# A decode kernel's last weights: w_down cut into sixteen blocks, the second half of wo into six pieces

## The chip, the core and the metric

The kernel runs on one core of one Trainium2 chip. The metric is device time in microseconds of one execution. Three unprofiled runs of the kernel before took 1313.51, 1313.98 and 1314.48 us; their median, 1313.98 us, is the time before.

## What is computed

One token of each of four sequences goes through an attention block with a cached history and, beside it, through a gated feed-forward block; a learned gate mixes the two. All data are 32-bit floats. Cut to what matters:

```python
# x [4, 1, 512]; k_cache, v_cache [4, 32, 4096, 128]; wq [512, 4096]; wo [4096, 512]
# w_gate, w_up [512, 1792]; w_down [1792, 512]; gate_w [512]
g = sigmoid((x * gate_w).sum(-1, keepdims=True))
q = (x @ wq) split into 32 heads of 128
p = softmax(q @ k_cache^T / sqrt(128))
a = (p @ v_cache, heads joined) @ wo
b = (gelu_tanh(x @ w_gate) * (x @ w_up)) @ w_down
out = g * a + (1 - g) * b
```

The two caches are 268 MB each, so nearly all of the 565 MB that the kernel reads is cache.

## The kernel before

**Tiles.** A tile is four heads of one sequence: 4096 positions of four heads lie as 128 partitions by 128 positions by 128 numbers, 64 KB in each partition, 8 MB in all. There are NT = 32 such tiles of K and 32 of V. Everything that comes from memory lands in one large array, `big`, whose stretches are reused: `K(i)` and `V(i)` give the stretch for tile i, and neighbouring K tiles overlap in a quarter, which is why each K tile is worked through in a `shared` quarter and a remaining three quarters. VectorE multiplies K by the query (`products`, L213) and sums (`sums`, L219), ScalarE makes the exponentials (`soft_max`, L237 and L240), TensorE multiplies by V (`pv`, L272).

**Order.** The order of the instructions is written out by hand (`tc.manual_schedule()`), engine by engine in program order. Every load is issued by SyncE's queue (SP), in program order: an issue that must wait for a stretch of `big` to become free holds back all issues behind it. The loop issues K(i+1) after the first quarter of tile i has been summed, and V(i) after `pv(i-1)`.

**The feed-forward block.** Up and gate projections run in the first tile of the loop (`ffn_up`, `ffn_gelu`). The result lies as 128 partitions by 448 columns: partition group j of 32 holds the rows of x for the features j·448 to j·448+447. VectorE transposes it in 14 strided selections of 32 columns (L349), so that `hT[:, i, :]` holds feature 14p+i in partition p. That fits `load_d` (L88), which puts rows 14p to 14p+13 of w_down into partition p as one run of 28 KB.

**The end.** After the loop SP issues `load_d`, then `load_w(0)` (L95, heads 0 to 15 of wo, 16 rows of 2 KB in each partition, in two pieces) and `load_w(1)` (heads 16 to 31, in four pieces of 9, 4, 2 and 1 rows, as `WO_END` says). w_down and the first half of wo go into the stretch of V(30), which `pv(30)` frees; the second half of wo goes into the stretch of K(31), which the last `sums` frees. TensorE then does, in this order: `pv(31)`, the gathering of the last heads, `ffn_down` (into `wide`, L254), the transposes of `turn(1)` (L307), the sixteen products of wo's first half (also into `wide`), `fold` (ScalarE copies `wide`, L264, and TensorE adds its four groups into `acc`), and the sixteen products of wo's second half (into `acc`, L259, four each). VectorE copies `acc` out (L413) and SP stores it (L414).

Of the kernel before, what the change touches and what calls it, by code (L numbers as in the profile page):

```python
# [9 lines left out]
F32 = mybir.dt.float32  # L10
# [7 lines left out]
def tile_gated_mix(ctx: ExitStack, tc: tile.TileContext, x, kc, vc, wq, wo, w_gate, w_up, w_down, gate_w, out):  # L18
    nc = tc.nc
    P = 128  # L20
    B, H, S, D = kc.shape
    DM = x.shape[2]
    F = w_gate.shape[1]
# [9 lines left out]
    RJ = 4  # L33
    BP = 2
    FG = F // 4
    FC = F // P
    HW = 16
    E = HW * D // P
    GW = HW // HT
    WO_END = ((0, E // 2, E), (0, 9, 13, 15, E))  # L40
    scale = 1.0 / math.sqrt(D)
    c_gelu = math.sqrt(2.0 / math.pi)

# [8 lines left out]
    consts = ctx.enter_context(tc.tile_pool(name="consts", bufs=1))  # L52
# [9 lines left out]
    big = kv.tile([P, VA + TW], F32)  # L62
    Q0, F0, F1, W0, D0 = VA, VA, VA + KC * F, VA, VA + TW // 2
    W1, ES = TW, TW + TW // 2

    def place(a, n):
        return big[:, a:a + n]
# [17 lines left out]
        nc.sync.dma_start(place((F0, F1)[s], KC * F), (w_gate, w_up)[s].rearrange("(p c) n -> p (c n)", c=KC))  # L85

    def load_d():
        nc.sync.dma_start(place(D0, FC * DM), w_down.rearrange("(p i) n -> p (i n)", i=FC))  # L88

    def load_w(w):  # L90
        t = place((W0, W1)[w], E * DM)
        src = wo[w * HW * D:(w + 1) * HW * D].rearrange("(p e) n -> p (e n)", e=E)
        ends = WO_END[w]
        for e0, e1 in zip(ends, ends[1:]):
# [149 lines left out]

    acc = ps1.tile([P, C4], F32, name="acc")
    wide = ps1.tile([P, DM], F32, name="wide")
    NW = FC + E
    nw = iter(range(NW))


    def project_wide(t, w):
        n = next(nw)
        c = n % 4
        nc.tensor.matmul(wide[32 * c:32 * c + 32, :], t, w, start=n < 4, stop=n >= NW - 4)  # L254

# [69 lines left out]


    hT = consts.tile([P, FC, 32], F32)
    fu = place(VA + 2 * KC * F, 2 * DM).rearrange("p (s n) -> p s n", s=2)

    def ffn_up(s):  # L330
# [7 lines left out]
    def ffn_gelu():  # L338
        x1 = fu[:, 0, :FG]
        t1, t2, t3, th, y, v = (place(F1 + a * DM, FG) for a in range(6))  # L340
        nc.vector.tensor_tensor(t1, x1, x1, op=OP.mult)  # L341
        nc.vector.tensor_scalar(t2, t1, 0.044715, 1.0, op0=OP.mult, op1=OP.add)  # L342
        nc.vector.tensor_tensor(t3, t2, x1, op=OP.mult)  # L343
        nc.scalar.activation(th, t3, AF.Tanh, scale=c_gelu)  # L344
        nc.vector.scalar_tensor_tensor(y, th, 1.0, x1, op0=OP.add, op1=OP.mult)  # L345
        nc.vector.scalar_tensor_tensor(v, y, half, fu[:, 1, :FG], op0=OP.mult, op1=OP.mult)  # L346

        for i in range(FC):
            nc.vector.transpose(hT[:, i, :], v[:, i::FC])  # L349

    def ffn_down():
        for f in range(FC):
            project_wide(hT[:, f, :], place(D0 + f * DM, DM))


    load_f(0)
# [2 lines left out]
    for i in range(NT):  # L359
# [12 lines left out]
        if i == 0:  # L372
            half, gmask = gates()
            ffn_up(0)
            ffn_up(1)
            ffn_gelu()
            load_v(0)
# [14 lines left out]
        if b == 1 and g + 1 < NG:  # L392
            q_spread(g + 1)
    load_d()
    load_w(0)
    load_w(1)
# [4 lines left out]
    gather(NG - 1)  # L401
    weigh(NG - 1)
    ffn_down()
    turn(1)
    turned(1)
# [31 lines left out]
```

## Time and profile before

| what | us |
|---|---|
| median of three runs (lowest, highest) | 1313.98 (1313.51, 1314.48) |
| the profiled execution, its own time | 1314.19 |
| its span, from the first instruction to the last | 1312.4 |
| DMA in the span: 565.07 MB, mean rate | 431 GB/s |
| VectorE busy, share of the span | 1143.1, 87% |
| TensorE busy, share of the span | 394.1, 30% |
| w_down, from issue to landing | 18.1 |
| the four pieces of wo's second half, from issue to landing | 27.8 (first), 30.6 and 30.7 (last two) |

The profile's page and the answers of the trace give times from the start of the span; the profiled execution lasted 1.8 us longer than its span. A window's row gives, in this order: the stretch, its length, the busy time and number of instructions of PE (TensorE matmul), PEld (weight load), DVE (VectorE), ACT (ScalarE) and POOL, the granted TensorE clock, the busy share of the 16 DMA engines and what they moved. A row of the timeline has start, duration, engine, line, operation, output and inputs with shapes, and in brackets how long the engine had been idle and what ended that.

### The profile page before, as it was taken

The numbers are of one execution on the slowest core, as the hardware profiler recorded it, in microseconds if no ns is written. First come the engines' busy times: TensorE is split into PE (matmuls) and PEld (weight loads), VectorE is DVE, ScalarE is ACT, GpSimd is POOL, SyncE is SP. The second block draws the span as 40 slices with busy tenths as digits, with TensorE's granted clock in tenths as the row PEclk, the third lists the DMA queues.
The fourth block names the chain that finished last, engine by engine and source line by source line (L and its number), as shares of the span: only waits on it lengthen the run. The fifth ranks groups of instructions, "written<-read, shape, count | busy, mean of one in ns | idle before, by whom it ended". The sixth has DMA issues, their size and how long they took to land.

```text
span 1312.4 us, 6364 instructions
## 1 busy us (share of the span) xinstructions
PE 394.1 (30%) x2728; PEld 132.3 (10%) x2728; DVE 1143.1 (87%) x261; ACT 92.7 (7%) x321; POOL 0.7 (0%) x6
## 2 busy tenths in 40 slices
PE   2403323322233221333232233322123332123237
PEld 0100001000011000100011000100001000010003
DVE  1799989988899988988989988998889899898890
ACT  0010000000000100000000000000000000000010
POOL 0000000000000000000000000000000000000000
PEclk9656666556666655666655666665566665566668
DMA  9999999999999999999999999999999999999997
GB/s 416 432 432 440 423 440 423 442 433 435 436 428 435 434 433 435 436 431 430 434 442 430 436 428 437 432 433 438 429 439 424 442 431 434 441 422 440 431 426 335
DMA packets 10855, 565.07 MB, mean 431 GB/s; under 512 B 1336, under 2 KB 1352, under 8 KB 1612
## 3 DMA queue, kind: packets, MB, share of 16 engines
q1 hardware_dynamic: 10828, 564.68, 99.4%
q8 instruction: 21, 0.34, 0.1%
q14 instruction: 6, 0.05, 0.0%
HBM read 564.67 MB, written 0.01 MB: 430 GB/s over the span
## 4 chain that ended last, share of the span: by engine, by line
DMA 71%; DVE 28%; PE 0%; issue 0%; SPq 0%; ACT 0%; DVEq 0%
DMA big<-in_A_k_cache 69%; DVE big L213 14%; DVE sc L219 14%; DMA big<-in_A_wo 2%; PE acc L259 0%; DVE m L233 0%; DVE hT L349 0%; DVE big L346 0%; DVE big L341 0%; DVE big L343 0%; DVE big L345 0%; ACT big L344 0%; DVE m L226 0%; DVE t L313 0%; DVE big L342 0%
## 5 line engine op out<-in xcount | busy, mean ns | idle before, releaser
L213 DVE TENSOR_TENSOR big<-big,qb 128x4096 f32<-128x4096 f32 x64 | 555.8, 8684 | 104.2 <-DMA big<-in_A_k_cache 104.2
L219 DVE TENSOR_REDUCE sc<-big 128x32 f32<-128x4096 f32 x64 | 555.4, 8678 | 1.1
L272 PE MATMUL po<-big,PM 128*32 128x512 f32 x2048 | 296.0, 743 | 437.0 <-DMA big<-in_A_v_cache 434.6
L272 PEld LDWEIGHTS po<-big,PM 128*32 128x32 f32 x2048 | 80.7, 133 | 626.0 <-issue 623.5
L235 PE MATMUL sm<-m,ones 1*128 1x4 f32 x64 | 18.7, 360 | 217.9 <-DVE m L233 217.9
L228 PE MATMUL sm<-ident,m 128*1 128x128 f32 x32 | 11.9, 371 | 213.9 <-DVE m L226 180.2
L240 ACT ACTIVATE PM<-sc,nb 32x128 f32<-32x128 f32 x128 | 67.4, 526 | 2.5
L237 ACT ACTIVATE nb<-sm 128x4 f32<-128x4 f32 x32 | 5.6, 174 | 570.8 <-PE sm L235 570.8
L235 PEld LDWEIGHTS sm<-m,ones 1*128 1x128 f32 x64 | 15.9, 306 | 237.6 <-DVE m L233 237.6
L281 ACT ACTIVATE o<-po 128x512 f32<-128x512 f32 x16 | 9.6, 597 | 324.2 <-PE po L272 324.2
L228 PEld LDWEIGHTS sm<-ident,m 128*1 128x1 f32 x32 | 2.5, 79 | 236.4 <-issue 183.3
L240 ACT ACTIVATION_READ_ACCUMULATOR PM<-sc,nb 32x1 f32 x128 | 26.2, 205 | 0.0
L200 ACT ACTIVATE qb<-q 128x512 f32<-128x512 f32 x8 | 4.8, 597 | 245.3 <-PE q L196 245.3
L128 DVE COPY xT<-sm 128x128 f32<-128x128 f32 x4 | 0.9, 282 | 20.4 <-PE sm L125 20.4
L196 PE MATMUL q<-QM,hmask 128*32 128x512 f32 x64 | 14.6, 1004 | 3.5 <-DVE QM L186 3.5
L289 PE MATMUL sm<-o,sel 128*16 128x128 f32 x128 | 15.6, 273 | 0.0
L334 PE MATMUL q<-big,xT 128*32 128x448 f32 x64 | 10.4, 813 | 9.3 <-DMA big<-in_B_w_gate 4.9
L299 DVE RECIPROCAL ri<-sm 16x1 f32<-16x1 f32 x8 | 1.2, 147 | 13.4 <-PE sm L291 13.4
L289 PEld LDWEIGHTS sm<-o,sel 128*16 128x16 f32 x128 | 11.7, 97 | 7.4 <-issue 5.0
L413 DVE COPY res<-acc 128x128 f32<-128x128 f32 x1 | 0.3, 291 | 13.2 <-PE acc L259 13.2
L226 DVE TENSOR_REDUCE m<-sc 128x1 f32<-128x128 f32 x32 | 9.2, 286 | 1.1
L233 DVE TENSOR_REDUCE m<-sm 1x4 f32<-1x128 f32 x32 | 8.7, 272 | 0.6 <-PE sm L228 0.6
(61 smaller groups left out, 79.2 us busy)
## 6 DMA issues: line engine op xcount, KB each, us to landing
big<-in_A_wo SPq DMA_DIRECT2D x2, 2048.0 KB, 25.0
big<-in_B_w_gate SPq DMA_DIRECT2D x1, 3584.0 KB
big<-in_B_w_up SPq DMA_DIRECT2D x1, 3584.0 KB, 27.6
big<-in_B_w_down SPq DMA_DIRECT2D x1, 3584.0 KB, 18.1
big<-in_A_wo SPq DMA_DIRECT2D x1, 2304.0 KB, 27.8
big<-in_A_wo SPq DMA_DIRECT2D x1, 1024.0 KB
big<-in_A_k_cache SPq DMA_DIRECT2D x32, 29.6
big<-in_A_v_cache SPq DMA_DIRECT2D x32, 29.2
```

Of the source, the lines that this page charges most:

```text
L196: nc.tensor.matmul(ps[h * PH:(h + 1) * PH].rearrange("p b d -> p (b d)"), hmask[:, j, a:a + 1].to_broadcast([P, PH]), QM.rearrange("p b d ...
L213: nc.vector.tensor_tensor(t, t, QB[g][:, b:b + 1, :].to_broadcast([P, r1 - r0, D]), op=OP.mult)
L219: nc.vector.tensor_reduce(SC[i][:, r0:r1], K(i).rearrange("p (r d) -> p r d", d=D)[:, r0:r1], axis=AX.X, op=OP.add)
L226: nc.vector.tensor_reduce(m1, SC[i], axis=AX.X, op=OP.max)
L228: nc.tensor.transpose(MT[i], m1, ident)
L233: nc.vector.tensor_reduce(m2, MT[i].rearrange("o (h p) -> o h p", h=HT), axis=AX.X, op=OP.max)
L235: nc.tensor.matmul(nbp, ones[:1, :], m2, start=True, stop=True)
L240: nc.scalar.activation(PM[:, PZ:].rearrange("p (c m) -> p c m", m=32)[s, :, h:RJ * HT:HT], SC[i][s, :].rearrange("p (c j) -> p c j", j=RJ) ...
L272: nc.tensor.matmul(PO[i // BP % 2][32 * c:32 * c + 32].rearrange("p j d -> p (j d)"), PM[:, m0:m0 + 32], V(i)[:, j * N:(j + 1) * N], start ...
L281: nc.scalar.activation(O[i // BP], PO[i // BP % 2], AF.Copy)
L289: nc.tensor.matmul(OS[g][:, :D], sel[:, j, m0:m0 + B * HT], O[N * g + n][:, j, :], start=(n, j) == (0, 0), stop=(n, j) == (N - 1, RJ - 1))
L334: nc.tensor.matmul(ps[32 * j:32 * j + 32, :], xT[:, c, :32], place((F0, F1)[s] + c * F + j * FG, FG), start=c == 0, stop=c == KC - 1)
```

## The change

w_down's 1792 rows are seen as NE = 16 blocks of FB = 112 rows. Block e belongs to partitions 8e to 8e+7. Of each block the first 96 rows are loaded as before, as one load of all blocks, 12 consecutive rows in each of the 8 partitions (24 KB a partition). The last 16 rows of each block come by two more loads, one for blocks 0 to 7 and one for blocks 8 to 15, 2 rows in each of 8 partitions for each block. Both of these loads go to partitions 0 to 63, side by side in a free stretch at the end of K(31)'s place (`DX`). So partitions 0 to 63 receive 16 rows each, and partitions 64 to 127 receive 12, where all received 14.

The transposes and the products follow: 12 transposes and products over 128 partitions, and 4 over 64 (`hX`), in place of 14 over 128. The second half of wo comes in pieces of 4, 4, 3, 2, 2 and 1 rows in place of 9, 4, 2 and 1.

```diff
-    FC = F // P
+    NE, EP = 16, 8
+    FB = F // NE
+    XR = 2
+    FC = FB // EP - XR
+    XP, XC = P // 2, 2 * XR
...
-    WO_END = ((0, E // 2, E), (0, 9, 13, 15, E))
+    WO_END = ((0, E // 2, E), (0, 4, 8, 11, 13, 15, E))
...
+    DX = ES + 4 * DM
...
     def load_d():
-        nc.sync.dma_start(place(D0, FC * DM), w_down.rearrange("(p i) n -> p (i n)", i=FC))
+        blocks = w_down.rearrange("(e f) n -> e f n", f=FB)
+        nc.sync.dma_start(place(D0, FC * DM), blocks[:, :EP * FC].rearrange("e (p i) n -> e p (i n)", i=FC))
+        for k in range(2):
+            nc.sync.dma_start(place(DX + k * XR * DM, XR * DM)[:XP],
+                              blocks[k * EP:(k + 1) * EP, EP * FC:].rearrange("e (p i) n -> e p (i n)", i=XR))
...
-    NW = FC + E
+    NW = FC + XC + E
...
+    hX = consts.tile([XP, XC, 32], F32)
...
+        v = v.rearrange("r (e f) -> r e f", f=FB)
+        main = v[:, :, :EP * FC].rearrange("r e (p i) -> r e p i", i=FC)
+        rest = v[:, :, EP * FC:].rearrange("r e (p i) -> r e p i", i=XR)
         for i in range(FC):
-            nc.vector.transpose(hT[:, i, :], v[:, i::FC])
+            nc.vector.transpose(hT[:, i, :], main[:, :, :, i])
+        for k in range(2):
+            for i in range(XR):
+                nc.vector.transpose(hX[:, k * XR + i, :], rest[k * XP:(k + 1) * XP, :, :, i])
...
     def ffn_down():
         for f in range(FC):
             project_wide(hT[:, f, :], place(D0 + f * DM, DM))
+        for f in range(XC):
+            project_wide(hX[:, f, :], place(DX + f * DM, DM)[:XP])
```

## The prediction

> **What bounds the kernel now.** I read the page first: the span, the DMA row of the 40 slices and the queue table, then the chain of waits.
>
> ```profile
> span 1312.4 us, 6364 instructions
> DMA  9999999999999999999999999999999999999997
> q1 hardware_dynamic: 10828, 564.68, 99.4%
> q8 instruction: 21, 0.34, 0.1%
> DMA 71%; DVE 28%; PE 0%; issue 0%; SPq 0%; ACT 0%; DVEq 0%
> ```
>
> The DMA engines are full from the first slice to the last but one. VectorE's 28% of the chain is no second bound: it passes between the landing of one K tile and the issue of the next, while the engines still work off a V tile. The windows give the rate, in the bulk and while w_down arrives.
>
> ```profile
> 135.70:1256.50 1120.80, 322.36 (x2133) 104.81 (x2133) 1020.70 (x191) 78.86 (x282) 0.00 (x0) 0.62 1.00 434
> 1280.20:1288.60 8.40, 8.20 (x64) 2.21 (x65) 0.00 (x0) 0.15 (x2) 0.00 (x0) 0.82 0.98 421
> ```
>
> 434 GB/s over 16 engines is 27.1 GB/s for one. The change moves the same bytes, so only two things can alter the time: how evenly the engines finish, and whether the new loads keep that rate. The end, in windows of 1 us:
>
> ```profile
> 1302.00:1303.00 1.00, 0.00 (x0) 0.00 (x0) 0.00 (x0) 0.00 (x0) 0.00 (x0) 1.00 0.98 410
> 1303.00:1304.00 1.00, 0.00 (x0) 0.00 (x0) 0.00 (x0) 0.00 (x0) 0.00 (x0) 0.85 0.83 342
> 1304.00:1305.00 1.00, 0.96 (x20) 0.88 (x24) 0.00 (x0) 0.00 (x0) 0.00 (x0) 0.50 0.62 256
> 1305.00:1306.00 1.00, 1.00 (x28) 0.89 (x24) 0.00 (x0) 0.00 (x0) 0.00 (x0) 0.50 0.51 209
> 1306.00:1307.00 1.00, 1.00 (x24) 0.91 (x20) 0.00 (x0) 0.00 (x0) 0.00 (x0) 0.50 0.48 182
> 1307.00:1308.00 1.00, 1.00 (x44) 0.98 (x38) 0.00 (x0) 0.00 (x0) 0.00 (x0) 0.94 0.17 64
> ```
>
> Half of the engines stop between 1303 and 1305.2; the other half (share 0.51, then 0.48) go on until 1306 to 1307.9. So there is an early half and a late half; the slowest of the early ones is done about 2.7 us before the last of the late ones. The second thing to see is that 8 engines alone move 209 GB/s, 26 each: those that are left do not speed up. The limit belongs to each engine or to its way into the memory; it is no common pool from which others make a loss good.
>
> The late half sets the end through these rows (issues with their time to landing, then the timeline):
>
> ```profile
> big<-in_B_w_down SPq DMA_DIRECT2D x1, 3584.0 KB, 18.1
> big<-in_A_wo SPq DMA_DIRECT2D x1, 2304.0 KB, 27.8
> big<-in_A_wo SPq DMA_DIRECT2D x1, 256.0 KB, 30.7
> L95 SPq DMA_DIRECT2D big<-in_A_wo x6: 328/428/434, 1270.9 to 1277.5; - x6
> ...
> 1263.21 12.95 DVE L219 TENSOR_REDUCE sc<-big 128x96 f32<-128x12288 f32 x1
> 1270.52 0.33 SPq L88 DMA_DIRECT2D big<-in_B_w_down  x1
> 1276.19 1.75 SPq L95 DMA_DIRECT2D big<-in_A_wo  x4
> 1290.51 3.60 PE L254 MATMUL wide<-big,hT 128*32 128x512 f32 x25
> 1298.58 1.92 PE L254 MATMUL wide<-big 128*32 128x512 f32 x16 [1.52 <-DMA big<-in_A_wo]
> 1300.57 0.60 ACT L264 ACTIVATE big<-wide 128x512 f32<-128x512 f32 x1 [3.79 <-PE wide L254]
> 1301.22 0.42 PE L259 MATMUL acc<-big,stack 128*32 128x128 f32 x8 [0.72 <-ACT big L264]
> 1304.04 5.18 PE L259 MATMUL acc<-big 128*32 128x128 f32 x128 [2.39 <-DMA big<-in_A_wo]
> 1308.82 0.40 PE L259 MATMUL acc<-big 128*32 128x128 f32 x8
> 1309.29 0.29 DVE L413 COPY res<-acc 128x128 f32<-128x128 f32 x1 [13.17 <-PE acc L259]
> ```
>
> The first piece of wo's second half (9 of 16 rows) lands at 1304.0; from there TensorE works 5.18 us without a gap and ends at 1309.22. The last piece lands at 1277.5 + 30.7 = 1308.2. So landing is 1.0 us ahead of TensorE's end, of which 0.4 us is work that only the last row allows (8 matmuls); 0.6 us is backlog from the large first piece.
>
> **The six pieces.** The first piece now has 4 rows, and no piece leaves more than 4 rows (32 of the 128 matmuls, 1.3 us) to do when it lands, while a row takes an engine 0.6 us to bring (16 KB): 3 rows, 1.8 us, follow the second 4, and every later piece has its work done, within 0.1 us, when the next lands. The backlog is gone when the last row lands; what remains is its 8 matmuls, 0.4 us, up to 0.7 at the halved clock of the windows 1304 to 1307. I take 0.5, so TensorE ends 0.5 us closer to the last landing. The two more issues on SP (0.44 us each, 1.75 for four) stand 20 us ahead of their data.
>
> **The small edits.** Two more transposes in the first tile cost 2 x 0.12 us and delay the issue of V(0) behind them:
>
> ```profile
> 32.51 0.33 SPq L85 DMA_DIRECT2D big<-in_B_w_up  x1
> 68.61 1.70 DVE L349 STREAM_TRANSPOSE hT<-big 128x32 f32<-128x32 f32 x14
> 70.46 0.33 SPq L76 DMA_DIRECT2D big<-in_A_v_cache  x1
> 1290.92 0.14 PEld L254 LDWEIGHTS wide<-big,hT 128*32 128x32 f32 x4 [0.29 <-issue]
> 1291.35 0.14 PEld L254 LDWEIGHTS wide<-big,hT 128*32 128x32 f32 x4 [0.29 <-issue]
> ...
> big<-in_B_w_up SPq DMA_DIRECT2D x1, 3584.0 KB, 27.6
> ...
> SPq L414 <- DMA big<-in_A_v_cache: 2.2, 1, 2.2
> ```
>
> K(1), queued behind w_up, which lands at 32.5 + 27.6 = 60.1, is 8.4 MB or 19.3 us of work for the engines, so they are busy to about 79, and V(0)'s issue at 70.7 costs nothing. Two more products in `ffn_down` are four matmuls, 0.43 us; the 1.52 us that TensorE waited for wo at 1298.58 hides them. The two small loads go to K(31)'s place, so they wait for the last sum (1263.21 + 12.95 = 1276.2), and both pieces of wo's first half, issued from 1270.9 on before, now queue behind them until about 1277.5. The engines are then still at V(31), and have w_down's main part (7.3 us) after it: nothing, unless the queue ran dry before 1287. The last row above shows the final store waiting for a V load's landing (V(31) is eight loads before it), which I read as an issue waiting for the landing of the load eight before it; with twelve loads outstanding the last wo pieces wait so too, some 10 us before their turn.
>
> **w_down's loads.** Before, an engine moves 3584 KB / 16 = 229 KB, 8.46 us at 27.1 GB/s (the window says 8.40). After, the main part is 12/14 of it, 7.25 us, and each small load is 32 KB for each of eight engines, 1.21 us, 2.42 for both. If the eight are the early half, it does 9.67 us (+1.21) and the late half 7.25 (-1.21). [...] No row here names an engine.
>
> What no row prices is the shape. Every large load of this trace writes 128 partitions from a source with one stride, and these run at 27.1 GB/s an engine. The new ones come in blocks of eight adjacent partitions, one block to an engine as I read the cut. If the fixed 27.1 GB/s is the engine's own, the shape costs nothing: 7.25 and 2.42 us, the lower end, as in the w_down row. If it is that of a way into the memory, the old shape gave each engine its own, and adjacent blocks need not: where two engines meet on one way, another stands empty and both run at half. The upper end is then twice the time, 14.5 and 4.84 us.
>
> From the upper end: the late half +6.04 (14.5 - 8.46); the early half +10.9 (14.5 + 4.84 - 8.46), less its lead of 2.7, so the last landing +8.2. Engines of one half are up to 1.9 us apart in the windows; two that meet with an offset go alone for that long, twice in a load. With a typical 0.75 us that gives back 1.5 us of the main part, and half of the small loads' surcharge, 1.2: +5.5 for the last landing. Between 5.5 and 8.2 I take +6.8. Between this and no cost at all I take it as the likelier: 434 GB/s is flat over 1120 us whatever VectorE and TensorE do and the remaining eight get no more, so there is no reserve that could absorb an uneven spread, and the trace's even rate belongs to another shape.
>
> [...]
>
> **Forecast (chance 0.66): the blocks get in each other's way.** Last landing 1308.2 + 6.8 = 1315.0, TensorE 0.5 us closer: +6.3. The profiled time 1314.19 becomes 1320.5; the median stands 0.2 below it, so 1320.3. Its own range: late half alone, 6.04 - 1.5 - 0.5 = +4, to the full 8.2: 1318.0 to 1322.2.
>
> **Rival 1, on the other side (0.26): the rate holds and the halves are evened out.** The late half's last landing moves from 1308.2 to 1307.0, the early half's to 1305.2 + 1.2, still ahead of it. Gain 1.2 + 0.5 = 1.7 us: 1312.3. For it: the tail's two halves fit the amount moved almost exactly. Against it: it needs the new shape to be free. It decides where the shape costs under 1.7 us.
>
> **Rival 2 (0.04): the eight are not the early half,** or the small loads spread over all 16. In the first case the late half gets +1.2, less 0.5: 1314.7; in the second only the 0.5 remains: 1313.5. The windows count engines and do not name them.
>
> **Rival 3 (0.04): more is evened out than the halves.** Idle engine time from 1303 to 1308 is 16 x (0.17 + 0.38 + 0.49 + 0.52 + 0.83) = 38 us, 2.4 us an engine; with the 0.5 that is 2.9: 1311.1. Against it: the pieces differ by 1.2 us steps and the spread inside each half stays.
>
> About 0.2% (2.6 us) is what a measurement of this kernel can tell from no change. The forecast is slower by more, rivals 1 and 2 lie within, rival 3 is faster by more: 0.66, 0.30, 0.04. The range reaches from rival 1 to the forecast's upper end, 1312.1 to 1322.3; this leaves out rival 3 and the tails.
>
> **What would show it.** Right: w_down's main part takes 12 to 14.5 us after V(31)'s landing at 1280.2 (7 us would refute it), DMA share or GB/s near half in the windows from 1280 to 1294, `ffn_down` starting after 1290.5 on a wait for w_down, and the last wo landing near 1315. In any case: TensorE's row at the end broken into pieces that wait for wo, and 0.4 to 0.7 us from the last landing to its end. For rival 1 the windows would stay above 0.9 until 1305 and fall within 2 us. If SP's issue of wo shows an engine gap before 1287, the queue order was the fault instead.

## The result, and the profile after

| | us |
|---|---|
| before: median (lowest, highest) of 4 runs | 1314.02 (1313.51, 1314.48) |
| after: median (lowest, highest) of 4 runs | 1329.50 (1326.92, 1330.13) |
| after over before, with its 95% interval | 1.0113 [1.0100, 1.0125] |
| the profiled execution after, its span | 1330.13, 1328.4 |

The change costs 15.5 us. The direction was forecast (slower, chance 0.66), but the time lies above the range, 7.2 us over its upper end of 1322.3. The forecast's surcharge was 6.3 us, so the loss was two and a half times as large.

From the page of the changed kernel: span, the DMA row in 40 slices with its rate below, and the queue table.

```profile
span 1328.4 us, 6378 instructions
DMA  9999999999999999999999999999999999999997
GB/s 411 441 438 417 442 435 418 443 434 438 423 443 430 437 428 443 426 439 432 437 428 441 426 439 432 439 426 437 436 437 426 435 440 437 424 437 434 442 287 259
q1 hardware_dynamic: 11260, 564.68, 99.3%
```

The rate row of the kernel before:

```profile
GB/s 416 432 432 440 423 440 423 442 433 435 436 428 435 434 433 435 436 431 430 434 442 430 436 428 437 432 433 438 429 439 424 442 431 434 441 422 440 431 426 335
```

The DMA row is digit for digit that of before, and the bytes are the same. Only the rate row tells what happened: 287 and 259 GB/s in the last two slices (33 us each), where they had 426 and 335. Slow packets keep the busy row as full as quick ones: in the 28.2 us from 1275.8 on, quoted below, the share is 0.97 at 223 GB/s, and before it was 0.98 at 418. A reader who had only the busy row would have found nothing.

Windows through the end of the changed kernel (busy time by engine, then the granted TensorE clock, the DMA share and GB/s):

```profile
1256.50:1275.80 19.30, 8.89 (x64) 2.46 (x64) 19.27 (x2) 0.00 (x0) 0.00 (x0) 0.77 1.01 429
1275.80:1280.20 4.40, 0.95 (x3) 0.57 (x3) 1.24 (x3) 2.45 (x9) 0.00 (x0) 0.50 1.05 214
1280.20:1284.00 3.80, 0.00 (x0) 0.00 (x0) 0.00 (x0) 0.46 (x2) 0.00 (x0) 0.50 0.91 175
1284.00:1288.00 4.00, 0.87 (x7) 0.27 (x11) 0.00 (x0) 0.00 (x0) 0.00 (x0) 0.50 0.95 203
1292.00:1296.00 4.00, 4.00 (x40) 1.22 (x36) 0.00 (x0) 0.00 (x0) 0.00 (x0) 0.99 1.00 210
1296.00:1300.00 4.00, 2.44 (x26) 1.66 (x18) 0.90 (x2) 0.60 (x1) 0.00 (x0) 1.00 0.97 223
1300.00:1304.00 4.00, 3.19 (x28) 0.82 (x28) 0.00 (x0) 0.00 (x0) 0.00 (x0) 1.00 0.97 328
1275.80:1304.00 28.20, 15.45 (x113) 5.63 (x113) 2.13 (x5) 3.51 (x11) 0.00 (x0) 0.71 0.97 223
1304.00:1316.00 12.00, 7.27 (x48) 2.07 (x48) 0.84 (x2) 0.63 (x1) 0.00 (x0) 0.72 0.99 413
1316.00:1320.00 4.00, 3.28 (x36) 0.89 (x32) 0.00 (x0) 0.60 (x1) 0.00 (x0) 0.57 0.69 279
1320.00:1324.00 4.00, 3.12 (x100) 2.31 (x92) 0.00 (x0) 0.00 (x0) 0.00 (x0) 1.00 0.11 43
```

The same 28.2 us of the kernel before, and its tail:

```profile
1275.80:1304.00 28.20, 19.95 (x169) 7.30 (x169) 2.66 (x7) 4.73 (x13) 0.00 (x0) 0.86 0.98 418
1304.00:1308.00 4.00, 3.96 (x92) 3.67 (x96) 0.00 (x0) 0.00 (x0) 0.00 (x0) 0.61 0.44 178
```

Half rate (175 to 223 GB/s in these windows) begins at 1275.8, while V(31) is still arriving, and lasts until 1300; the share stays above 0.9. Over the 28.2 us the changed kernel moves 223 GB/s in place of 418: it lost 28.2 x (1 - 223/418) = 13.2 us of transfers. The rest is at the finish, where some engines have nothing left to do. From 1304 on, before, the engines' mean idle time was 4 x 0.56 = 2.2 us; after, from 1316 on, it was 4 x 0.31 + 4 x 0.89 = 4.8 us. Together 13.2 + 2.6 = 15.8, which is the difference of the two profiled executions (1330.13 - 1314.19 = 15.9) to 0.1 us.

The issues with their time to landing, and SyncE's waits:

```profile
big<-in_B_w_down SPq DMA_DIRECT2D x1, 3072.0 KB, 31.6
big<-in_A_v_cache SPq DMA_DIRECT2D x1, 36.3
...
SPq L106 <- DMA big<-in_B_w_down: 17.6, 3, 13.4
SPq L106 <- DMA big<-in_A_v_cache: 7.3, 1, 7.3
```

The row of V(31) in the kernel that has only the six pieces (first experiment below):

```profile
big<-in_A_v_cache SPq DMA_DIRECT2D x1, 29.9
```

w_down's main part, 14% smaller than the load before, takes 31.6 us in place of 18.1. The second row is V(31), whose shape was not touched: 36.3 us in place of 29.9. So a load in the old shape was slowed by what ran beside it. The single packets show it too. V(31) comes in packets of 64 KB; those begun up to 1274 run at 27.1 GB/s, all but one at 22.5, and the last, begun from 1276 on, at 9 to 14. The timeline of TensorE at the end (in brackets the idle time and what ended it):

```profile
1287.13 9.52 PE L283 MATMUL po<-big,PM 128*32 128x512 f32 x64 [8.86 <-DMA big<-in_A_v_cache]
1300.81 2.78 PE L265 MATMUL wide<-big,hT 128*32 128x512 f32 x24 [2.37 <-DMA big<-in_B_w_down]
1305.66 1.05 PE L265 MATMUL wide<-big,hX 64*32 64x512 f32 x4 [1.09 <-DMA big<-in_B_w_down]
1310.23 3.64 PE L265 MATMUL wide<-big 128*32 128x512 f32 x16 [2.43 <-DMA big<-in_A_wo]
1315.08 3.64 PE L265 MATMUL wide<-big 128*32 128x512 f32 x16 [1.21 <-DMA big<-in_A_wo]
1322.99 0.64 PE L270 MATMUL acc<-big 128*32 128x128 f32 x16 [0.37 <-DMA big<-in_A_wo]
1324.23 1.06 PE L270 MATMUL acc<-big 128*32 128x128 f32 x24 [0.60 <-DMA big<-in_A_wo]
```

From V(31) on, one step after another now waits for a landing. The last row holds the last 24 matmuls, 16 of the fifth piece and 8 of the sixth; they end at 1325.29, against 1309.22 before.

### The profile page after: what moved, and what is told of

Read it like the earlier page. It is cut to its first block, busy times and chain, and to the rows that moved or that the text cites. A ratio compares the mean times of both kernels' runs of the same rounds, so it can differ in the third digit from the quotient of the medians.

```text
span 1328.4 us, 6378 instructions
## 1 busy us (share of the span) xinstructions
PE 399.9 (30%) x2732; PEld 132.6 (10%) x2732; DVE 1143.5 (86%) x263; ACT 92.6 (7%) x321; POOL 0.7 (0%) x6
## 4 chain that ended last, share of the span: by engine, by line
DMA 71%; DVE 28%; issue 0%; PE 0%; SPq 0%; ACT 0%; DVEq 0%
DMA big<-in_A_k_cache 68%; DVE big L224 14%; DVE sc L230 14%; DMA big<-in_B_w_down 2%; DMA big<-in_A_wo 2%; DVE m L244 0%; DVE hT L364 0%; PE acc L270 0%; DVE big L358 0%; DVE big L355 0%; DVE big L357 0%; DVE big L353 0%; ACT big L356 0%; DVE m L237 0%; DVE hX L367 0%
## 5 line engine op out<-in xcount | busy, mean ns | idle before, releaser
L246 PEld LDWEIGHTS sm<-m,ones 1*128 1x128 f32 x64 | 15.9, 306 | 237.7 <-DVE m L244 237.7
L207 PE MATMUL q<-QM,hmask 128*32 128x512 f32 x64 | 15.5, 1061 | 3.5 <-DVE QM L197 3.5
L175 PE MATMUL po<-big,xT 128*32 128x512 f32 x64 | 9.8, 778 | 0.4 <-DVE xT L139 0.4
## 6 DMA issues: line engine op xcount, KB each, us to landing
big<-in_B_w_down SPq DMA_DIRECT2D x1, 3072.0 KB, 31.6
```

Source lines behind the costliest of these rows:

```text
L175: nc.tensor.matmul(PO[s][32 * j:32 * j + 32].rearrange("p j d -> p (j d)"), xT[:, c, :32], w[:, n0:n0 + HB * D], start=c == 0, stop=c == K ...
L207: nc.tensor.matmul(ps[h * PH:(h + 1) * PH].rearrange("p b d -> p (b d)"), hmask[:, j, a:a + 1].to_broadcast([P, PH]), QM.rearrange("p b d ...
L246: nc.tensor.matmul(nbp, ones[:1, :], m2, start=True, stop=True)
```

## The experiments

Two explanations of the halved rate, called theories here, went into the first runs. **Theory W (ways)** supposes that each engine has its own way into the memory only while it writes its own partitions, and that blocks of eight adjacent partitions send engines onto each other's ways; no row names a way. **Theory S (source):** the memory that is read minds sixteen streams 224 KB apart. A third is that blocks as a form are slow (a load cut in another way), wherever they land. A fourth is the queue order. All ratios are to the kernel before, measured beside each set; its median there was 1314.36 (the first four kernels), 1314.25 (the four with added loads of several sizes) and 1314.24 us (the last three).

### The six pieces alone

```diff
-    WO_END = ((0, E // 2, E), (0, 9, 13, 15, E))
+    WO_END = ((0, E // 2, E), (0, 4, 8, 11, 13, 15, E))
```

> The kernel before with wo's second half in six pieces and nothing else. Both theories of the slow loads (ways: engines whose blocks of eight adjacent partitions share ways into the memory; source: sixteen engines reading places 224 KB apart meet on the reading side) say the same: w_down and wo keep their rate, last landing near 1308.2 as before, TensorE ends 0.4 to 0.7 us behind it in place of 1.0. Time 1313.5 (1313.2 to 1314.0). If the smaller pieces themselves were slow, the last landing would come later than 1308.5.

1313.62 us, 0.9993 [0.9985, 1.0002]. Timeline of its TensorE:

```profile
1301.51 1.06 PE L259 MATMUL acc<-big 128*32 128x128 f32 x32
1303.51 1.08 PE L259 MATMUL acc<-big 128*32 128x128 f32 x32 [0.93 <-DMA big<-in_A_wo]
1305.33 0.86 PE L259 MATMUL acc<-big 128*32 128x128 f32 x24 [0.74 <-DMA big<-in_A_wo]
1306.54 0.65 PE L259 MATMUL acc<-big 128*32 128x128 f32 x16 [0.36 <-DMA big<-in_A_wo]
1307.78 1.07 PE L259 MATMUL acc<-big 128*32 128x128 f32 x24 [0.59 <-DMA big<-in_A_wo]
```

The unbroken 5.18 us of before falls into pieces that wait for their rows, and TensorE ends at 1308.85, 0.47 us behind the last landing (1308.38) in place of 1.0. The profile shows half a microsecond less between landing and end; in the median, 0.7 us lower, the interval just includes no change.

### The same blocks, source rows close together

```diff
-        nc.sync.dma_start(place(D0, FC * DM), blocks[:, :EP * FC].rearrange("e (p i) n -> e p (i n)", i=FC))
+        nc.sync.dma_start(place(D0, FC * DM), w_down[:P * FC].rearrange("(p e i) n -> e p (i n)", e=NE, i=FC))
```

> The changed kernel, with the main part of w_down still cut in sixteen blocks of eight adjacent partitions, but its source rows beside one another: engine e reads 12 rows at 12e + 192p, so that the sixteen read within 384 KB at any time. (The rows go to other partitions than the reference needs.) Theory ways: nothing changes, w_down's main part takes 13 to 15 us, the rate from 1277 to 1300 stays at 200 to 215 GB/s, time 1328 to 1331. Theory source: the main part takes 7 to 8 us at 400 GB/s or more, only the small loads (still 224 KB apart) may be slow, time 1312 to 1317.

1326.56 us, 1.0089 [1.0075, 1.0103]. Two windows:

```profile
1284.00:1288.00 4.00, 1.61 (x8) 0.45 (x12) 0.00 (x0) 0.00 (x0) 0.00 (x0) 0.50 0.99 209
1292.00:1296.00 4.00, 4.00 (x41) 1.62 (x34) 0.00 (x0) 0.60 (x1) 0.00 (x0) 1.00 1.01 213
```

The engines write the main part into the same partitions from sources 24 KB apart, and the rate is halved all the same (209 and 213 GB/s): theory S falls for the main part. Whether it is truly quicker than the change (the two intervals, 1.0075 to 1.0103 and 1.0100 to 1.0125, still touch) was not followed up.

### The main part plain, the small loads in blocks

```diff
-        nc.sync.dma_start(place(D0, FC * DM), blocks[:, :EP * FC].rearrange("e (p i) n -> e p (i n)", i=FC))
+        nc.sync.dma_start(place(D0, FC * DM), w_down.rearrange("(p i) n -> p i n", p=P)[:, :FC].rearrange("p i n -> p (i n)"))
```

> The changed kernel with only the main part made plain (128 partitions with one stride, 12 of every 14 rows); the two small loads stay as in the change, eight blocks of eight adjacent partitions each, 224 KB apart. (The main part's rows go to other partitions than the reference needs.) It prices the small loads alone. Theory ways: they take up to twice 2.4 us on the early half, and with its lead of 2.7 us the last landing is 0 to 2.4 us later than with four quarters: 1312.3 to 1315. Theory source: the same range, as they are 224 KB apart too. If the time is above 1320, the small loads and not the main part are the cause of the loss.

1319.22 us, 1.0030 [1.0017, 1.0044], above what was expected. Its windows:

```profile
1284.00:1288.00 4.00, 4.00 (x40) 1.09 (x36) 0.00 (x0) 0.00 (x0) 0.00 (x0) 0.91 0.98 240
1288.00:1292.00 4.00, 4.00 (x42) 2.11 (x38) 0.47 (x2) 0.60 (x1) 0.00 (x0) 1.00 0.94 249
1292.00:1296.00 4.00, 4.00 (x29) 0.73 (x21) 0.43 (x1) 0.00 (x0) 0.00 (x0) 1.00 1.01 390
```

V(31) arrives in time again (TensorE works through 1284 to 1292, and every packet of V(31) runs at 27.1 GB/s), but the two small loads, 512 KB, hold the rate at 240 to 249 for 8 us. Of the 15.5 us, the main part's shape accounts for 1329.5 - 1319.2 = 10.3.

### Main part plain, the rest in groups of four partitions

```diff
-        for k in range(2):
-            nc.sync.dma_start(place(DX + k * XR * DM, XR * DM)[:XP],
-                              blocks[k * EP:(k + 1) * EP, EP * FC:].rearrange("e (p i) n -> e p (i n)", i=XR))
+        tails = w_down.rearrange("(j a e i) n -> j e a i n", j=4, a=4, e=8)[:, :, :, FC:]
+        for j in range(4):
+            nc.sync.dma_start(place(DX + j // 2 * XR * DM, XR * DM)[32 * (j % 2):32 * (j % 2) + 32],
+                              tails[j].rearrange("e a i n -> e a (i n)"))
```

The main part is plain as in the kernel just shown, and the transposes select accordingly.

> The same bytes moved to the same side, in another shape: main part as one load of 128 partitions with one stride (the first 12 of every 14 rows), and the last two rows of each 14 by four loads of eight engines by four partitions (partitions 0-31, 32-63, 0-31, 32-63), so that each engine writes four partitions of its own; six pieces of wo. Theory ways: no engine meets another, full rate; the late half ends 1.2 us earlier; time 1312.3 (1311.8 to 1313.2). Theory source: the main part is free too, the small loads read 14-row steps, also free: the same time. If the eight engines that take the small loads are not the early half: 1314.5 to 1316.

1314.74 us, 0.9999 [0.9991, 1.0008].

```profile
1284.00:1288.00 4.00, 4.00 (x32) 1.07 (x28) 0.00 (x0) 0.00 (x0) 0.00 (x0) 0.75 0.99 417
1288.00:1292.00 4.00, 4.00 (x45) 2.09 (x41) 0.00 (x0) 0.60 (x1) 0.00 (x0) 1.00 1.03 434
1304.00:1308.00 4.00, 1.37 (x40) 0.97 (x40) 0.00 (x0) 0.00 (x0) 0.00 (x0) 1.00 0.45 176
```

As many bytes go into the same 64 partitions, in blocks of four adjacent partitions in place of eight, and the rate is full (417 and 434 GB/s): the small loads' shape was worth 1319.2 - 1314.7 = 4.5 us. (They also come from other source rows, in four loads in place of two, so this pair alone does not say what in the shape did it.) What did not come is the evening-out: the tail's share, 0.45, is that of the six pieces alone (0.45 in the same window). By the landing events (in the changed kernel's trace sixteen for w_down's main part and, from 1293.1 on, eight for each small load; one is taken to stand for one engine), the eight that carry the small loads are not the early half: six of them were early, two late, and two early engines got nothing.

### Added loads: how many engines, how many partitions each

The kernel before, with extra loads of w_down rows into a free stretch that nothing reads, behind the last sum. This is measured apart from any change of w_down.

```diff
+        ENG, PER, LOADS = 8, 4, 8     # 8, 8, 4;  4, 8, 4;  4, 16, 2 in the other three
+        blocks = w_down.rearrange("(e f) n -> e f n", e=16)[:ENG]
+        groups = P // (ENG * PER)
+        for m in range(LOADS):
+            p0, c0 = m % groups * ENG * PER, ES + 4 * DM + m // groups * 2 * DM
+            nc.sync.dma_start(place(c0, 2 * DM)[p0:p0 + ENG * PER],
+                              blocks[:, m * 2 * PER:(m + 1) * 2 * PER].rearrange("e (p i) n -> e p (i n)", i=2))
```

> The kernel before with 1 MB more to load between w_down and wo: eight loads in which each of eight engines writes 4 KB into each of four adjacent partitions (32 partitions a load, sources 224 KB apart); nothing reads them. [...] Time 1317 to 1320. Theory form (a source with two counts, or one 224 KB apart, is slow by itself): each load takes 1.2 us, time 1323 or more.

> The same 1 MB on the same eight engines from the same rows in the same order, but each engine writes eight adjacent partitions (four loads over 64 partitions). [...] Theory form: the same time as with four partitions, within 1 us.

> The kernel before with 512 KB more: four loads in which each of four engines writes 4 KB into each of eight adjacent partitions (32 partitions a load, 128 KB an engine in all). [...] Theory adjacent (an engine that writes eight adjacent partitions is slow by itself, or slows the others): 2 to 2.4 us a load, the rate falls, time 1319 to 1323.

> The same 512 KB on the same four engines from the same rows, each engine writing sixteen adjacent partitions (two loads over 64 partitions). [...] Theory adjacent: like the load with eight partitions.

A block is taken to be one engine's share. Theory W expected 1317 to 1320, 1323 to 1328, 1314 to 1317 and 1319 to 1324 us, in the order of the table.

| engines x partitions each, total | us | ratio | GB/s, DMA share in 1284 to 1294 |
|---|---|---|---|
| 8 x 4, 1 MB in eight loads | 1320.68 | 1.0049 [1.0026, 1.0071] | 226, 0.68 |
| 8 x 8, 1 MB in four loads | 1326.04 | 1.0090 [1.0061, 1.0119] | 252, 1.02 |
| 4 x 8, 512 KB in four loads | 1319.87 | 1.0037 [1.0017, 1.0057] | 265, 0.99 |
| 4 x 16, 512 KB in two loads | 1321.47 | 1.0057 [1.0035, 1.0080] | 248, 1.00 |

8 x 8 fell into the range of theory W, and its time is 5.4 us above that of 8 x 4, where the theory of the form had them within 1 us. 8 x 4 is a miss for theory W: its time lies just above that range, but its rate is 226 GB/s, and 400 or more had been expected. The author had asked only whether the eight meet one another; half of their loads go to partitions 64 to 127, where such loads are slow, as the next pair of kernels shows (219 GB/s in place of 416). And 8 x 4 hides a second effect, in its windows and SyncE's waits:

```profile
1288.00:1290.00 2.00, 2.00 (x23) 0.48 (x14) 0.00 (x0) 0.00 (x0) 0.00 (x0) 1.00 0.46 158
1290.00:1292.00 2.00, 2.00 (x26) 1.61 (x25) 0.01 (x1) 0.60 (x1) 0.00 (x0) 1.00 0.24 94
SPq L94 <- DMA big<-in_B_w_down: 9.1, 1, 9.1
```

Here the share falls as well: the engines had nothing to do, since an issue waited 9.1 us for the landing of the load eight before it, and wo's issues stood behind it. 4 x 8 was expected at full rate by theory W and ran at 265 GB/s: a second miss. Its time fell into the range of the other theory, that an engine which writes eight adjacent partitions is slow for that alone. Two of the four loads go to partitions 64 to 127, which can be argued afterwards to be the cause. These four kernels do not separate the theories; the next pair shows what the partitions alone do.

### The same load into the lower or the upper partitions

```diff
+        ENG, PER, FIRST = 8, 4, 0     # 64 in the other
+        blocks = w_down.rearrange("(e f) n -> e f n", e=16)[:ENG]
+        for m in range(4):
+            p0, c0 = FIRST + m % 2 * ENG * PER, ES + 4 * DM + m // 2 * 2 * DM
+            nc.sync.dma_start(place(c0, 2 * DM)[p0:p0 + ENG * PER],
+                              blocks[:, m * 2 * PER:(m + 1) * 2 * PER].rearrange("e (p i) n -> e p (i n)", i=2))
```

> The kernel before with 512 KB more between w_down and wo: four loads in which eight engines write 4 KB into each of four adjacent partitions, all in partitions 0 to 63, from rows 224 KB apart; nothing reads them. [...] Theory form (loads with a block count in the source are slow): the rate falls below 300 for some 5 us; time 1318 to 1322.

> The same four loads, the same engines, rows, sizes and order, but into partitions 64 to 127. [...] Theory form: the same time as with partitions 0 to 63, within 0.7 us.

Theory W expected 1315.5 to 1317.5 us and more than 390 GB/s for the lower partitions, 1318 to 1322 us and 200 to 260 GB/s for the upper ones.

Into partitions 0 to 63: 1315.89 us, 1.0013 [1.0002, 1.0023]. Into 64 to 127: 1320.46 us, 1.0049 [1.0033, 1.0064]. The same window of the kernel before, of the lower kernel, then of the upper one:

```profile
1284.00:1294.00 10.00, 10.00 (x94) 3.71 (x86) 0.89 (x2) 0.60 (x1) 0.00 (x0) 1.00 0.98 416
```

```profile
1284.00:1294.00 10.00, 10.00 (x94) 3.75 (x86) 0.89 (x2) 0.60 (x1) 0.00 (x0) 1.00 0.98 416
```

```profile
1284.00:1294.00 10.00, 7.70 (x74) 3.15 (x70) 0.90 (x2) 0.60 (x1) 0.00 (x0) 0.99 0.99 219
```

Sources, bytes, shape, number and order of the loads are the same; only the partitions differ by 64. One runs at the rate of the kernel before in that window (416), the other at 53% of it. For these loads the target partitions decide, and neither the block form nor the source nor the order of the queue does: all three are in the lower kernel too, which runs at the full rate.

### One engine off its way

```diff
+        nc.sync.dma_start(place(ES + 4 * DM, 4 * DM)[64:81], w_down[:17 * 4].rearrange("(p i) n -> p (i n)", i=4))
```

The kernel before with one more load between w_down and wo, 17 partitions (64 to 80) by 8 KB, 139 KB in all; it is taken to run on one engine, as its 17 packets, strung together below, are one chain of 9.3 us. "Meeting" is theory W's word for two engines on one way.

> [...] If meeting slows only the two that meet: the total stays at 380 GB/s or more; the one engine ends 5 to 10 us later, time 1316 to 1322. If one meeting slows all sixteen, as the earlier runs suggest: the total falls to 200 to 300 GB/s for about 10 us, 1320 to 1324.

1319.10 us, 1.0037 [1.0023, 1.0051]. The time lies in the range for a meeting that slows only two; the rate lies between the two expectations.

```profile
1284.00:1294.00 10.00, 10.00 (x95) 3.85 (x89) 0.89 (x2) 0.60 (x1) 0.00 (x0) 0.95 0.97 369
```

Were only one pair of engines halved, 15/16 of 416 would be left, 390 GB/s; 369 were. In the single packets from 1284.6 to 1293, two engines at a time ran at 12 to 16 GB/s, which are taken to be the one with the added load and one that it meets; the others ran at 27 at first and at some 22 to 26 from 1288.5 on.

Packets that follow one another without a gap can be strung together to one engine's work. The engine with the added load took 9.3 us for its 17 packets, where 139 KB take 5.1 at 27.1 GB/s. It had done its part of V(31) 4.3 us before the last engine, and it was the last to finish. So here the end is late by its own slow time less its lead, 9.3 - 4.3 = 5.0; the other fifteen lost only some 0.5 to 2 us each.

## Why the prediction was right and wrong

**The bound and the seeing of it: right.** The loss lies in the rate of the DMA engines (223 GB/s in place of 418 over the 28.2 us); the share stays near 1 (0.97).

**The mechanism: right in kind.** By the prediction, "where two engines meet on one way, another stands empty and both run at half". That the target partitions alone halve the rate is what the pair of lower and upper partitions shows (416 and 219 GB/s). In the change, w_down's main part runs at 12.9 to 13.7 GB/s in the middle half of its packets, as forecast; plain, in the kernel with four quarters, it runs at 26.9. That engines meet in pairs, and which ones, is argued, not shown: no row names an engine or a way. The 1.21, 2.42 and 4.84 us of the small loads take each of them to run on eight engines; no row before showed that. In the changed kernel's trace the main part has sixteen landing events, and each small load eight from 1293.1 to 1305.6 (and one 1.1 us after its issue, which is too early for 32 KB at 27.1 GB/s). In order of time, the second small load's eight stand 1.9 to 2.7 us behind the first's, about the 2.42 us of one load at half rate.

**The size: wrong, and this is the step that failed.** The prediction charged the half rate to the new loads alone: 14.5 us for the main part, 4.84 us for a half's small loads, less 2.7 us of lead and 2.7 us that offsets were to give back. That assumed that the half rate holds for the new loads only, for their own time, and that an engine's lead comes off it. In place of that, all that arrived between 1275.8 and 1300 went at half rate: the rest of V(31) (its last packets at 9 to 14 GB/s), the main part, the small loads, and the first rows of wo (11.6 to 18.6), though the shapes of V(31) and wo were not touched.

- The shape of the main part was to cost 14.5 - 7.25 - 1.5 = 5.75 us. It cost 10.3 (the main part made plain). The engines that came early to their blocks slowed those still at V(31): it landed 6.4 us later after its issue (36.3 in place of 29.9), half rate began at 1275.8, not at 1280.2, and with the main part plain no packet of V(31) is slow. So in the change the lead gave nothing back; being ahead only began the clash sooner. The prediction's window for half rate was 1280 to 1294, 14 us; it lasted from 1275.8 to 1300, 24 us.
- The shape of the small loads was to add 4.84 - 2.42 = 2.42 us, less 1.2 for the offsets. It cost 4.5 us between the two runs that differ in the small loads alone. That they slow engines which carry none of them was left out: eight engines at half would leave 12/16 of 416, 312 GB/s, and 240 to 249 were measured with the main part plain.
- Engines finish further apart: 4.8 us of mean idle time at the end in place of 2.2. No term stood for that. It follows the clash in time; that the clash causes it is argued.

The kernel with a single engine off its way sets this apart. There the prediction's reckoning holds: the engine's own slow time less its lead (9.3 less 4.3) is what the end is late, and the others lose little. It fails in the change, where the whole rate is near half (223 GB/s in place of 418).

**The six pieces: right.** TensorE ends about 0.5 us behind the last landing, as forecast: 0.47 us in the run that has them alone.

**The small edits: right.** No step but those that wait for data is late. The issue that waits for the landing eight loads before it is confirmed: by the waits quoted above, wo's issues stood 7.3 + 17.6 = 24.9 us in all behind landings. SyncE's row of these issues:

```profile
1277.86 28.10 SPq L106 DMA_DIRECT2D big<-in_A_wo  x8
```

The last of them was out at 1306.0. The wait was harmless, since the share stays near 1 until 1316 (0.99 from 1304 on). In the kernel of 8 x 4 such a wait starved the engines (share 0.24).

**What would show it.** The main part landed at 1269.2 + 31.6 = 1300.8, 13.7 us after V(31) (1287.1), inside the 12 to 14.5 forecast; but V(31) itself was late, and the prediction took its landing as given at 1280.2. `ffn_down` waited 2.37 us for w_down, as said. The last landing was at 1324.8 by its event, not 1315.

**Rival 1 (rate holds, halves evened: 1312.3)** was tried with a shape that does hold the rate: 1314.74 us. Its rate part is possible with that shape; its evening-out is not what such loads of eight engines do, as **rival 2** had it, with 1314.7 for that case: the eight are not the early half, by six to two. Which engines are late in a run, and whether others could be picked, stays open. No run bears out **rival 3**.

**What stays open.** Meetings in pairs do not explain all of the loss. Four engines off their ways can halve eight at most, which would leave 12/16 of 416 = 312 GB/s; 265 and 248 were measured. Why the rate falls below that was not found. Nor do these runs separate the ways from a further cost of eight adjacent partitions: the upper kernel shows that the rate is near half with four adjacent ones as well (219 GB/s), not that eight cost nothing more. No version here beats the kernel before by more than its measurement can tell; the six pieces alone are the nearest, with 0.7 us and an interval that includes none.

## What to carry to other kernels

Where a load's pieces landed halved the rate of all that was under way here (219 GB/s in place of 416), and a full busy row (share 0.99) didn't show it: look at GB/s beside the share. When reshaping a load on a DMA-bound path, keep the plain form over all partitions that the large loads have (w_down's main part ran at 26.9 GB/s an engine in it, at 12.9 to 13.7 in blocks), or measure the new shape alone. Price a clash for every load under way at that time, the untouched ones too (V(31) landed 36.3 us after its issue in place of 29.9). Small loads that even out engines must be aimed at the engines that are late, and the windows do not name them.

## What the runs showed of the hardware

- The target partitions alone halved the rate: 416 GB/s with added loads of eight blocks, four partitions each, in 0 to 63, and 219 with the same loads in 64 to 127.
- One added load of 17 partitions, taken to run on one engine, slowed more than one other engine: 369 GB/s in place of 416, where a halved pair alone would leave 390.
- Slowed transfers showed as long packets (64 KB at 9 to 14 GB/s in place of 27.1) and a full share: share 0.97 with 223 GB/s over 28 us after, 0.98 with 418 before.
- SyncE's issues waited for the landing of the load eight before them, 24.9 us in all in the changed kernel. With eight small loads in the queue such a wait of 9.1 us left the engines idle: share 0.46, then 0.24. (The traces have eight semaphores that tell of landings, so the wait can be the program's own.)
